# Attention of a fused RWKV, soft-MoE and feed-forward kernel rebuilt: one load per unit, natural keys by TensorE, decay table in PSUM, even and odd chunks as steps, w_in in quarters

## The chip, the cores and the metric

The kernel runs on one core of a Trainium2 chip. The metric is the device time of one execution in microseconds (us); the time given is the median of three runs.

## The reference, cut to what matters

Attention with a decaying state, then a soft mixture of experts, then a feed-forward block with squared ReLU. `w_in` and `w_out` come as float64, everything else as float32.

```python
# r, k, v: [4, 8, 768, 48]; w, u: [8, 48]
for t in range(S):
    cur = np.einsum('bhd,bhe->bhde', u[None] * kt, vt)
    y[:, :, t] = np.einsum('bhd,bhde->bhe', rt, state + cur)
    state = w[None, :, :, None] * state + np.einsum('bhd,bhe->bhde', kt, vt)
# x = y as [3072 tokens, 384]; 8 experts of 4 slots, F = 1024
logits = x @ phi
slot_input = softmax(logits over tokens).T @ x
slot_out[e] = relu(slot_input[e] @ w1[e]) @ w2[e]
x = softmax(logits over slots) @ slot_out
# d_ff = 2048
g = np.maximum(x @ w_in, 0) ** 2
out = g @ w_out
```

## The kernel before

**Units.** Attention is computed in 16 units, n = 0 to 15: one batch and a pair of heads each (four units make a batch). The 768 tokens of a unit are six chunks of 128. The turned arrays r and k of a unit lie with the head dimension on the partitions (head h at 64h to 64h+47), in `t_view`; the natural ones, k and r (`n_view`) and v (`vs`), with the tokens on the partitions. The host lays them out, and each comes by loads of its own: two of the turned arrays per unit (line 91), one of natural k and r (95), one of v (98), all on SP's queue from unit 1 on. Four units are in flight in `slot0` to `slot3`.

**One unit's work.** `decay` (231, VectorE) multiplies turned k and r by powers of w from the table `tab`. `prep` (238, 240, 242, GpSimd) forms r·u·k and weighs natural k with `pkn`. `weigh` (246, VectorE) sums r·u·k over a head's dimension, `diag` (253, GpSimd) spreads the sums on a diagonal in `AT`. `A` (263, TensorE) makes the products of k and r within a chunk, and a masked copy (265, VectorE) puts their upper triangles into `AT`. `KV` (274) makes k v per chunk, `scan` (280, VectorE) runs the state over the chunks, and ScalarE copies it into the block-diagonal `SBD` (284). `Y` adds state times r (294, full array, both heads at once) and `AT` times v (299). `X` (310, 311) transposes the result into `xn`, `L` (320) gives the logits. A unit is done in two steps g of three chunks each. At a batch's end `soft1a` to `soft3` and `softc` follow.

**Float64 to float32.** `to_f32` (137, 139, 141) takes the two words of a float64 apart in three VectorE instructions. All of `w_in` is loaded (146) and converted within the attention loop, 16 blocks of 128 x 384, at one block a unit (`conv_win`). `w_out` is loaded (154) and converted (to `wf`) and split into two fp32r parts (612, 617) during the expert stage and the first feed-forward steps.

**Order.** Instructions are issued in the order in which the program writes them (a manual schedule); each engine works in that order, and semaphores tie them. Seven expert weights (176, 179) are loaded in the loop in slots 6 to 12, four more in the units' slots as the last units end.

**Behind the loop.** A pass over the softmax of the last batch, then eight experts (`up` 556, `turn` 566, `down` 574), then `G` (678) and `quarters` (695) make the feed-forward's first factor `gst`; quarters 512 to 2047 go through `gq` and SP's transfers (708) to their partitions. Then come 96 steps i of nine matrix instructions (805), with `s_h` (722), `s_relu` (734, ScalarE), `s_sq` (739 ScalarE, 741 VectorE), `s_hi` (744, ScalarE), `s_lo` (747, VectorE) two and one steps ahead; step i belongs to f = i // 2 modulo 16.

Of the kernel before, what the change touches and what calls it, by code (L numbers as in the profile page):

```python
# [17 lines left out]
def rwkv_softmoe_ffn(ctx: ExitStack, tc: tile.TileContext, tr, kr, vn, wt, u, phi, w1, w2, w_in, w_out, out):  # L30
    nc = tc.nc
    NU, _, D, _, S = tr.shape
    NP = wt.shape[1]
    H = 2 * NP
    B = NU // NP
    NC = S // 128
    DM, NTOK = out.shape
# [47 lines left out]
    def n_view(n):

        return units[n % NB][:, 2 * S:2 * S + 4 * NC * D].rearrange("p (m c h d) -> p m c h d", m=2, c=NC, h=2)

    def load_t(n, engs, cols=slice(0, NC)):
        for h in range(2):  # L90
            engs[h].dma_start(t_view(n)[64 * h:64 * h + D, :, cols],
                              tr[n, h].rearrange("d m (c t) -> d m c t", c=NC)[:, :, cols])

    def load_n(n, eng=nc.sync):
        eng.dma_start(n_view(n).rearrange("p m c h d -> p m (c h d)"), kr[n].rearrange("p m c h d -> p m (c h d)"))

    def load_v(n, eng=nc.sync):
        eng.dma_start(vs[n % NV].rearrange("p c h d -> p (c h d)"), vn[n].rearrange("p c h d -> p (c h d)"))

    base = const.tile([112, 8], F32, name="base")  # L100
    nc.sync.dma_start(base[:, :NP], wt)
    nc.vector.memset(units[0][32:64, :2 * S], 0.0)
    load_t(0, (nc.sync, nc.scalar), slice(0, GC))
    load_n(0)
    load_t(0, (nc.sync, nc.scalar), slice(GC, NC))
    U = att.tile([128, NP, 2, D], F32, name="U")
# [313 lines left out]
    for j in range(3):  # L420
        prep(1, j)
# [444 lines left out]
```

## Time and profile before

| | us |
|---|---|
| median of three runs | 455.57 (453.97 to 457.31) |
| span of the profiled execution | 451.8 |
| PE busy | 397.7 |
| DVE busy | 308.9 |
| ACT busy | 209.2 |
| POOL busy | 135.0 |

The span is one execution from its first to its last instruction, taken by the hardware profiler; the median also holds what lies around it. PE is the matrix part of TensorE, PEld its weight loads, DVE VectorE, ACT ScalarE, POOL GpSimd, SP the queue that issues most loads. A busy time is an average over stages that are bounded by different things, so it has to be read by stage. fp32 matrix products appear as two instructions each, transposes as one. The granted clock is a share of 2.4 GHz.

### The profile page before, as it was taken

The numbers are of one execution on the slowest core, as the hardware profiler recorded it, in microseconds if no ns is written. First come the engines' busy times: TensorE is split into PE (matmuls) and PEld (weight loads), VectorE is DVE, ScalarE is ACT, GpSimd is POOL, SyncE is SP. The second block draws the span as 40 slices with busy tenths as digits, with TensorE's granted clock in tenths as the row PEclk, the third lists the DMA queues.
The fourth block names the chain that finished last, engine by engine and source line by source line (L and its number), as shares of the span: only waits on it lengthen the run. The fifth ranks groups of instructions, "written<-read, shape, count | busy, mean of one in ns | idle before, by whom it ended". The sixth has DMA issues, their size and how long they took to land.

```text
span 451.8 us, 7475 instructions
## 1 busy us (share of the span) xinstructions
PE 397.7 (88%) x2917; PEld 300.9 (67%) x2917; DVE 308.9 (68%) x525; ACT 209.2 (46%) x390; POOL 135.0 (30%) x114
## 2 busy tenths in 40 slices
PE   3687747986598699899999999999999999999996
PEld 2565534764276466444788888888888888888884
DVE  6888997999898772424766575676555667555564
ACT  3142221332134334212598888665555565555553
POOL 7896772577279760000122122000000000000000
PEclk9699996969599889999999999999999999999999
DMA  7989997699749987997243220030000012000004
GB/s 196 265 241 307 296 323 176 191 312 299 213 94 316 303 311 244 316 390 265 83 128 104 72 89 16 1 140 1 0 0 2 0 42 100 0 1 0 0 2 140
DMA packets 28516, 67.59 MB, mean 150 GB/s; under 512 B 2848, under 2 KB 12832, under 8 KB 28480
## 3 DMA queue, kind: packets, MB, share of 16 engines
q1 hardware_dynamic: 28112, 66.61, 48.4%
q10 hardware_dynamic: 368, 0.49, 0.5%
q8 instruction: 23, 0.38, 0.3%
q14 instruction: 13, 0.11, 0.1%
HBM read 61.59 MB, written 4.72 MB: 147 GB/s over the span
## 4 chain that ended last, share of the span: by engine, by line
PE 69%; DVE 14%; issue 4%; POOL 3%; DMA 2%; ACT 2%; SPq 0%; DVEq 0%; ACTq 0%; POOLq 0%
PE ps_A L805 22%; PE ps_lg L805 7%; PE ps_kv L805 7%; PE ps_Y L805 7%; PE ps_tr L722 5%; DVE AT L265 3%; DVE slot L231 3%; PE ps_Y L299 3%; PE ps_A L263 3%; DVE slot L139 2%; PE ps_Y L574 2%; PE ps_A L556 2%; PE ps_A L376 2%; DMA slot<-in_w_in_dram 2%; DVE dg L246 1%
## 5 line engine op out<-in xcount | busy, mean ns | idle before, releaser
L747 DVE TENSOR_TENSOR slot<-gg,slot 128x512 fp32r<-128x512 f32 (+1 forms) x97 | 66.5, 686 | 65.8 <-ACT slot L744 65.1
L805 PE MATMUL ps_A<-slot,slot 128*128 128x512 f32 x432 | 108.4, 395 | 0.0
L805 PEld LDWEIGHTS ps_A<-slot,slot 128*128 128x128 f32 x432 | 81.0, 188 | 19.4
L744 ACT CAST slot<-gg 128x512 fp32r<-128x512 f32 (+1 forms) x97 | 59.7, 616 | 50.7 <-DVE gg L741 49.9
L734 ACT ACTIVATE hr<-ps_tr 128x512 f32<-128x512 f32 (+1 forms) x97 | 57.5, 594 | 24.7 <-PE ps_tr L722 24.3
L741 DVE TENSOR_TENSOR gg<-hr 128x512 f32<-128x512 f32 (+1 forms) x71 | 48.9, 689 | 15.3 <-ACT hr L734 15.2
L805 PE MATMUL ps_lg<-slot,slot 128*128 128x512 f32 x144 | 56.0, 396 | 0.0
L805 PE MATMUL ps_Y<-slot,slot 128*128 128x512 f32 x144 | 56.0, 395 | 0.0
L805 PE MATMUL ps_kv<-slot,slot 128*128 128x512 f32 x144 | 55.9, 395 | 0.0
L253 POOL TENSOR_SCALAR_AFFINE_SELECT AT<-dg 128x768 f32<-128x768 f32 x32 | 34.2, 1070 | 49.8 <-DVE dg L246 47.7
L617 POOL TENSOR_TENSOR slot<-wf,slot 128x384 fp32r<-128x384 f32 x16 | 17.6, 1101 | 97.4 <-ACT slot L612 93.5
L231 DVE TENSOR_TENSOR slot<-slot,tab 112x768 f32<-112x768 f32 (+1 forms) x34 | 43.4, 1285 | 0.0
L299 PE MATMUL ps_Y<-AT,vs 128*48 128x128 f32 (+1 forms) x384 | 33.8, 291 | 10.1 <-DVE AT L265 9.8
L284 ACT COPY SBD<-sc 48x240 f32<-48x240 f32 x32 | 20.1, 629 | 43.4 <-DVE sc L280 43.2
L722 PE MATMUL ps_tr<-slot,slot 128*128 128x512 f32 x96 | 37.8, 395 | 0.0
L299 PEld LDWEIGHTS ps_Y<-AT,vs 128*48 128x48 f32 (+1 forms) x384 | 23.0, 134 | 17.9 <-DVE AT L265 14.9
L265 DVE COPY_PREDICATED AT<-mask,ps_A 128x384 f32<-128x384 int32 x64 | 33.5, 575 | 1.8 <-issue 1.6
L263 PE MATMUL ps_A<-slot 48*128 48x128 f32 x384 | 33.8, 315 | 0.0
L805 PEld LDWEIGHTS ps_Y<-slot,slot 128*128 128x128 f32 x144 | 27.0, 188 | 6.5
L805 PEld LDWEIGHTS ps_kv<-slot,slot 128*128 128x128 f32 x144 | 27.0, 188 | 6.4
L805 PEld LDWEIGHTS ps_lg<-slot,slot 128*128 128x128 f32 x144 | 27.0, 187 | 6.3
L240 POOL TENSOR_TENSOR slot<-slot 128x576 f32<-128x576 f32 x16 | 29.9, 1869 | 1.3
(154 smaller groups left out, 511.2 us busy)
## 6 DMA issues: line engine op xcount, KB each, us to landing
slot<-in_w_dram SPq DMA_DIRECT2D x14, 1536.0 KB, 12.9
slot<-in_kr_dram SPq DMA_DIRECT2D x16, 576.0 KB, 9.1
slot<-in_tr_dram SPq DMA_DIRECT2D x30, 288.0 KB, 8.6
slot<-in_w_in_dram SPq DMA_DIRECT2D x8, 768.0 KB, 10.0
wo<-in_w_out_dram SPq DMA_DIRECT2D x16, 384.0 KB, 3.1
vs<-in_vn_dram SPq DMA_DIRECT2D x16, 288.0 KB, 7.9
out_dram<-os SPq DMA_DIRECT2D x15, 256.0 KB, 2.1
post<-in_w_dram SPq DMA_DIRECT2D x2, 1536.0 KB, 8.4
```

What stands on the lines that cost most here:

```text
L231: eng.tensor_tensor(x, x, tab[:, n % NP, m].unsqueeze(1).to_broadcast([112, k_, 128]), ALU.mult)
L240: eng.tensor_tensor(rv, rv, kv, ALU.mult)
L253: nc.gpsimd.affine_select(out=at.rearrange("p c h t -> p (c h) t"), in_=dg.rearrange("p c h -> p (c h)").unsqueeze(2).to_broadcast([128, 2 ...
L263: nc.tensor.matmul(p[h][:, i], tv[rows, 1, GC * g + i], tv[rows, 0, GC * g + i], start=True, stop=True)
L265: nc.vector.copy_predicated(at[:, :, h], mask.unsqueeze(1).to_broadcast([128, GC, 128]), p[h])
L299: nc.tensor.matmul(p[64 * h:64 + D * h, i], vv[:, GC * g + i].rearrange("p h d -> p (h d)")[:, cols], at[:, i, h], start=False, stop=True, ...
L722: nc.tensor.matmul(p, gst[:, 128 * f:128 * (f + 1)], cTall[:, 512 * g:512 * (g + 1)], start=True, stop=True)
L734: nc.scalar.activation(fs[i, "hr"][:, c], fs[i, "p"][:, c], AF.Relu)
L741: nc.vector.tensor_mul(gg, hr, hr)
L744: nc.scalar.copy(part(i, "gh")[:, c], fs[i, "gg"][:, c])
L747: nc.vector.tensor_tensor(part(i, "gl")[:, c], fs[i, "gg"][:, c], fs[i, "gh"].bitcast(F32)[:, c], ALU.subtract)
L805: nc.tensor.matmul(o, (hi, lo, hi)[k][:, 128 * j:128 * (j + 1)], (gh, gh, gl)[k], start=(f == 0 and k == 0), stop=(f == NF - 1 and k == 2))
```

## The change

- The host joins turned r and k, natural r and natural v of a unit in one array `un` of 128 partitions x 2688 floats, three pieces of 896, zeros in the gaps. One DMA loads a unit; for unit 0 the three pieces go on three instructions (ScalarE's queue and SP's).
- Natural k is no longer loaded (except `k0` for unit 0, from GpSimd's queue): `kT` transposes the decayed turned k on TensorE, and ScalarE copies it to `kn`. The table factor that this carries is taken out of u instead (`UT`); the product with `pkn` goes.
- The table lies in PSUM, in one bank, and one half is read in reverse.
- A step is the even or the odd chunks of a unit. `A` writes one tile of two banks, and one masked copy of 768 elements does the work of two of 384. `SBD` and its copies go: `inter` multiplies the scanned state head by head (48 rows, 48 columns, 20 instructions for 10), `intra` does what line 299 did. Two Y banks stay allotted, and `X` writes its transposes into them. `L` has six products of 128 columns for three of 256.
- The softmax of a batch is spread over the first three units of the next; some of its copies go from VectorE to ScalarE; `xn` is doubled.
- `w_in` is loaded in quarters of 512 columns. Quarter 0 is converted in units 4 to 8, quarter 1 in the last units, quarters 2 and 3 in feed-forward steps 0 to 17, one instruction a step; their products (`quarters`) are made in steps 11 and 19, with 16 small transfers each.
- Weights in the loop are loaded in pieces of a third, `w2` is laid out by the host in runs of 4 KB.

The diff, cut to its core:

```diff
+    load_unit(0, (nc.scalar, nc.sync, nc.sync))
+    k0n = att.tile([128, NC, 2, D], F32, name="k0n")
+    nc.gpsimd.dma_start(k0n.rearrange("p c h d -> p (c h d)"), k0)
...
+    def conv_some(k):
+        for _ in range(k):
+            if conv:
+                q, c, i = conv.pop(0)
+                to_f32(win(q)[:, c], raws[q][:, c].rearrange("p (f t) -> p f t", t=2), (i,))
...
+    tabp = ps("tab")[:112].rearrange("p (a e) -> p a e", a=NP)
...
+    def decay(n, m, cols=slice(0, NC)):
         x = t_view(n)[:, m, cols]
+        t = tabp[:, n % NP, ::-1] if m else tabp[:, n % NP]
+        nc.vector.tensor_tensor(x, x, t.unsqueeze(1).to_broadcast(list(x.shape)), ALU.mult)
...
+    def kT(n, j):
+        tv = t_view(n)
+        p = ps("tr")[:, :HC * 128].rearrange("p (c e) -> p c e", c=HC)
+        for i in range(HC):
+            nc.tensor.transpose(p[:, i, :112], tv[:, 1, HC * j + i], ident[:112, :112])
         if j == 0:
+            st[n, "kn"] = wk([128, NC, 2, D], "kn", 2, pool=att)
+        nc.scalar.copy(st[n, "kn"][:, HC * j:HC * (j + 1)], heads(p))
...
+    def cp(n, par):
+        nc.vector.copy_predicated(st[n, "AT", par], mask.unsqueeze(1).unsqueeze(1).to_broadcast([128, 2, HC, 128]),
+                                  st.pop((n, "A", par)))
...
+    def inter(n):
+        sc, tv = st.pop((n, "sc")), t_view(n)
+        for c in range(1, NC):
+            par = c % 2
             for h in range(2):
+                o = 64 * (h ^ par)
+                rows = slice(64 * h, 64 * h + D)
+                nc.tensor.matmul(y_view(par)[o:o + D, c // 2], sc[rows, :, c], tv[rows, 0, c], start=(c < 3), stop=True,
+                                 skip_group_check=True)
...
+        if nxt:
+            pr2(n + 1)
+        A(n, 1)
+        if nx2:
+            decay(n + 2, 1)
+        cp(n, 1)
+        if n > 0:
+            L(n - 1, 1)
+            X(n - 1, 1)
+            if hp == 0:
+                soft1a(prev)
+        if nxt:
+            KV(n + 1)
+            scan(n + 1)
+        if nx2:
+            pr1(n + 2)
+            kT(n + 2, 0)
+        inter(n)
+        if n > 0 and hp == 0:
+            soft1b(prev)
+        if nxt:
+            weigh(n + 1)
+            diag(n + 1, 0)
+        intra(n, 0)
+        if nx2:
+            kT(n + 2, 1)
+            decay(n + 2, 0)
+        if nxt:
+            A(n + 1, 0)
+            cp(n + 1, 0)
+            diag(n + 1, 1)
+        if n > NP - 1:
+            if hp == 0:
+                soft2(prev)
+            elif hp == 1:
+                softc(prev)
+            elif hp == 2:
+                soft3(prev)
+        intra(n, 1)
+        L(n, 0)
+        X(n, 0)
+        if n >= 4:
+            conv_some(2)
+        if n + NB < NU:
+            load_unit(n + NB)
...
+        if n == NU - 5:
+            conv_some(9)
+            load_win(1, 5)
+            conv_add(1)
...
+    load_win(2, 5)
+    load_win(3, FREE[7])
...
-        if i in (0, 2, 4):
-            quarter_out(1 + i // 2)
+        if i == 0:
+            conv_add(2)
+        if i == 9:
+            conv_add(3)
+        if i < 18:
+            conv_some(1)
+        if i in (11, 19):
+            quarters(2 + i // 19, "tr")
+            quarters_high()
+            quarters_low()
+            for j in range(NQ):
+                quarters_out(2 + i // 19, j)
```

## Rows read from the trace of the kernel before

**Rows 1.** Stretches: bounds, length, busy us (instructions) by engine, clock, DMA share, GB/s.

```profile
core 0: us, PE busy (x) PEld busy (x) DVE busy (x) ACT busy (x) POOL busy (x), PEclk, DMA share, GB/s
...
24.78:173.16 148.38, 114.32 (x1311) 83.65 (x1309) 129.09 (x202) 44.85 (x96) 97.23 (x71) 0.88 0.89 261
...
223.20:265.10 41.90, 41.90 (x184) 33.76 (x183) 28.19 (x53) 37.64 (x67) 10.05 (x9) 1.00 0.32 95
```

**Rows 2.** The same view for a plain unit, a batch's end and a late unit.

```profile
40.65:51.12 10.47, 7.90 (x92) 5.65 (x90) 10.33 (x15) 2.92 (x6) 7.26 (x6) 1.00 1.04 329
...
61.91:78.53 16.62, 9.36 (x85) 5.67 (x84) 12.88 (x24) 4.01 (x9) 8.25 (x7) 0.69 0.86 263
...
164.08:170.40 6.32, 6.32 (x95) 5.18 (x91) 5.44 (x8) 3.04 (x7) 4.28 (x5) 1.00 0.74 244
```

**Rows 3.** Groups by line: engine, operation, out<-in, count; busy us, mean ns; idle before.

```profile
L231 DVE TENSOR_TENSOR slot<-slot,tab 112x768 f32<-112x768 f32 x30 | 40.7, 1361 | 0.0
...
L265 DVE COPY_PREDICATED AT<-mask,ps_A 128x384 f32<-128x384 int32 x64 | 33.5, 575 | 1.8 <-issue 1.6
...
L139 DVE SCALAR_TENSOR_TENSOR slot<-slot,slot 128x384 int32<-128x384 int32 x16 | 14.9, 933 | 0.6
L141 DVE SCALAR_TENSOR_TENSOR slot<-slot,slot 128x384 int32<-128x384 int32 x16 | 14.4, 897 | 0.5
...
L280 DVE TENSOR_TENSOR_SCAN sc<-ps_kv,carry 112x288 f32<-112x288 f32 x16 | 12.0, 749 | 10.2 <-PE ps_kv L274 5.5 <-issue 2.6 <-ACT xT L303 2.1
L246 DVE TENSOR_REDUCE dg<-slot 128x12 f32<-128x576 f32 x16 | 11.9, 743 | 2.8 <-POOL slot L240 2.8
...
L137 DVE TENSOR_SCALAR slot<-slot 128x384 int32<-128x384 int32 x16 | 7.1, 443 | 2.1 <-DMA slot<-in_w_in_dram 2.1
```

**Rows 4.** Timeline of DVE and POOL: start, duration, engine, line, operation, idle before.

```profile
42.25 2.20 POOL L240 TENSOR_TENSOR slot<-slot 128x576 f32<-128x576 f32 x1
...
43.36 1.52 DVE L139 SCALAR_TENSOR_TENSOR slot<-slot,slot 128x384 int32<-128x384 int32 x1
...
48.46 0.56 DVE L139 SCALAR_TENSOR_TENSOR slot<-slot,slot 128x384 int32<-128x384 int32 x1
...
68.98 0.94 DVE L231 TENSOR_TENSOR slot<-slot,tab 112x768 f32<-112x768 f32 x1
```

**Rows 5.** Timeline of PE in the late unit.

```profile
164.08 0.94 PE L263 MATMUL ps_A<-slot 48*128 48x128 f32 x12
164.95 0.51 PE L310 MATMUL ps_tr<-ident,xT 112*128 112x112 f32 x3
165.29 0.82 PE L294 MATMUL ps_Y<-slot,SBD 112*112 112x128 f32 x6
166.04 0.87 PE L299 MATMUL ps_Y<-AT,vs 128*64 128x128 f32 x12
166.84 0.94 PE L263 MATMUL ps_A<-slot 48*128 48x128 f32 x12
...
169.85 0.62 PE L274 MATMUL ps_kv<-vs,slot 128*48 128x48 f32 x20
170.40 0.94 PE L263 MATMUL ps_A<-slot 48*128 48x128 f32 x12
```

**Rows 6.** Timeline of PE: A at the low clock, soft3 at the full one.

```profile
156.75 1.65 PE L263 MATMUL ps_A<-slot 48*128 48x128 f32 x12
...
183.27 1.50 PE L376 MATMUL ps_A<-xn,en 128*32 128x385 f32 x12 [0.20 <-DVE m L508]
```

**Rows 7.** Stretches within one unit: DMA share and GB/s are the last two columns.

```profile
44.00:47.00 3.00, 1.48 (x11) 0.94 (x9) 2.97 (x5) 0.40 (x1) 3.00 (x3) 1.00 1.01 415
47.00:51.00 4.00, 3.45 (x53) 3.08 (x53) 3.93 (x7) 0.48 (x1) 0.87 (x2) 1.00 1.06 213
```

**Rows 8.** Timeline of the feed-forward steps: SP's transfers, DVE waiting for ACT.

```profile
229.07 2.41 SPq L708 DMA_DIRECT2D slot<-gq  x4
...
231.06 0.69 DVE L747 TENSOR_TENSOR slot<-gg,slot 128x512 fp32r<-128x512 f32 x1 [1.52 <-ACT slot L744]
```

More of the change, by code (lines that the diff above doesn't have):

```diff
@@ L89, in load_t @@
[L89 to L98, printed above, removed]
@@ L124, in rwkv_softmoe_ffn, with win @@
+    st = {}
+    warm = const.tile([1, 4], F32, name="warm")
+    nc.gpsimd.memset(warm, 1.0)
+    nc.scalar.activation(warm[:, 0:1], warm[:, 1:2], AF.Exp)
     w_in32 = w_in.bitcast(I32)
     w_out32 = w_out.bitcast(I32)
-    raw = [t[:, 1536 * h:1536 * (h + 1)].rearrange("p (c f) -> p c f", c=3)
-           for t in (take(NSLOT - 2, I32), take(NSLOT - 1, I32)) for h in range(2)]
-    win = [take(i).rearrange("p (c f) -> p c f", c=3) for i in (4, 5)]
+    winslot = take(4)
+    raws = {}
+    def win(q):
+        return winslot[:, 1536 * (q % 2):1536 * (q % 2 + 1)].rearrange("p (c f) -> p c f", c=3)
@@ L131, in to_f32, with load_win @@
+    def load_win(q, slot, cs=range(3)):
+        if q not in raws:
+            raws[q] = take(slot, I32).rearrange("p (c f) -> p c f", c=3)
+        for c in cs:
+            nc.sync.dma_start(raws[q][:, c], w_in32[128 * c:128 * (c + 1), 1024 * q:1024 * (q + 1)])
     def to_f32(dst, words, steps=range(3)):
@@ L219, in keep_clock @@
+    xn = [att.tile([128, NC, DM + 1], F32, name=f"xn{i}") for i in range(2)]
     def keep_clock(n):
@@ new lines, in rwkv_softmoe_ffn @@
+    nc.scalar.copy(carry[:, :, :, 1:], pw[:, 1, :, 0].unsqueeze(2).unsqueeze(3).to_broadcast([112, NP, D, NC - 1]))
+    KV(0)
+    for par in range(2):
+        nc.vector.memset(YB[par][32:64, :HC * 128], 0.0)
+    cp(0, 0)
+    scan(0)
+    diag(0, 1)
+    uw = wk([112, NP], "uw", 1, pool=att)
+    rsc = wk([112, NP, 128], "xT", 2, pool=att)
+    nc.vector.tensor_mul(uw, base[:, :NP], base[:, NP:])
+    nc.vector.tensor_tensor(rsc, tabp, uw.unsqueeze(2).to_broadcast([112, NP, 128]), ALU.mult)
@@ L422, in rwkv_softmoe_ffn @@
-    for m in range(2):
-        decay(1, m)
-    loads = [[("win", n)] if n < NF // 2 else [] for n in range(NU - NB)]
-    for i, n in enumerate((1, 3, 5, 7, 9, 10, 11)):
-        loads[n].append(("w", i))
-    conv = []
+        nc.tensor.transpose(pp[:, a * 128:a * 128 + 112], rsc[:, a], ident[:112, :112])
+    nc.scalar.copy(UT, heads(pp.rearrange("p (a e) -> p a e", a=NP)))
+    for m in (1, 0):
+        decay(1, m)
+    pr1(1)
+    kT(1, 0)
+    kT(1, 1)
+    nc.gpsimd.memset(xn[0][:, :, DM:DM + 1], 1.0)
@@ L428, in rwkv_softmoe_ffn @@
+    nc.gpsimd.memset(xn[1][:, :, DM:DM + 1], 1.0)
+    loads = [[] for n in range(NU)]
+    pieces = [("w", 0, c) for c in range(3)] + [("x", 0, c) for c in range(3)]
+    pieces += [("w", i, c) for i in range(1, NEARLY) for c in range(3)]
+    for j, pc in enumerate(pieces):
+        loads[min(NU - NB - 1, j * (NU - NB) // len(pieces))].append(pc)
     for n in range(NU):
         nxt = n + 1 < NU
+        nx2 = n + 2 < NU
+        prev = n // NP - 1
+        hp = n % NP
         if n == 2:
@@ L767, in rwkv_softmoe_ffn @@
     quarters_low()
-    quarter_out(0)
+    for j in range(NQ):
+        quarters_out(1, j)
     s_sq(1)
```

458 lines of the change are left out of this document (197 added, 261 removed).

## The prediction

> **What bounds the kernel now.** Read the table of stretches first [rows 1]. The attention loop, from A of unit 1 (24.78 us) to A of the last unit (173.16 us), takes 148.4 us, 10.60 us for each of 14 units. DVE is busy for 129.09 us of it (87%), PE for 114.32, POOL for 97.23, and the 16 DMA engines for 0.89 of it at 261 GB/s. The granted clock there is 0.88. In the feed-forward steps (223.20 on) PE is busy throughout at the full level, 2.4 GHz, and DVE for 28.19 of 41.90. So the change must win in the loop and must not disturb the steps.
>
> Next, three single units [rows 2]. In a plain unit (40.65 to 51.12) DVE works 10.33 of 10.47 us: it is the bound. In a unit at a batch's end (61.91) 16.62 us go by, DVE works 12.88, PE 9.36, and the clock falls to 0.69. In a late unit, in which nothing is prepared or converted any more (164.08), PE works all 6.32 us: that is what PE needs for a unit today at the full clock.
>
> What DVE does is in [rows 3]: per unit two decays of 1361 ns, four masked copies of 575, one weigh (743), one scan (749) and the three steps of one conversion (443, 933, 897). The timeline says that some of these durations are waiting [rows 4]: the same L139 takes 1.52 us while POOL's L240 runs and 0.56 when POOL is idle; a decay takes 0.94 us at best. The masked copy, which reads one operand from PSUM, keeps its 575 ns throughout.
>
> **What the change costs and saves, DVE.** Decays: with the table in PSUM they read one SBUF operand, as the masked copy does. Bounds 0.94 and 1.36; I take the row they resemble, 0.95: 1.9 per unit, 0.8 less. Masked copies: two of 768 in place of four of 384; between 0.94 (the decay of 768 elements) and 2 x 0.575; I take 1.0, so 2.0. Weigh and scan stay: 1.5. Sum 5.4. Conversions: 16 blocks x 2.27 = 36.4 us fall to 17 steps of 512 elements within the loop (quarter 0 and eight steps of quarter 1). A step of 384 costs 0.76 on the mean, so 1.0 for 512; bounds 0.75 (0.56 scaled) and 2.0 (1.52 scaled). That is 17 us, 1.1 per unit. The softmax pieces cost 12.88 - 10.33 = 2.55 per batch, 0.6 per unit. DVE: 5.4 + 1.1 + 0.6 = 7.1 us per unit.
>
> **PE.** From start to start in the full-clock stretch [rows 5]: A of half a unit 0.87, transposes of half a unit 0.34, six instructions of L294 0.75, twelve of L299 0.80, KV 0.55; from 166.84 to 169.85, A, L, transposes, four of L294 and L299 leave 0.5 for L. New: kT, two more groups of transposes, 0.68 per unit. L294's ten full-array instructions (1.25) become twenty of 48 rows and 48 columns. No row shows these. At L299's rate (0.80 / 12 = 0.067) they cost 1.33; below it, the two row halves running side by side would give about 0.7; above it, at L294's rate of 0.125, 2.5. I take 1.33, as L299 has the same moving width and nearly the same weights. L has twice the instructions of half the width: 0.5 to 1.0, I take 0.65. Sum: 1.74 + 0.68 + 0.68 + 1.33 + 1.60 + 0.55 + 0.65 = 7.2. Per batch soft3, 1.50 at the full clock [rows 6], and two groups of transposes (0.3 each) add 2.1, so 0.5 per unit: 7.7.
>
> **The others.** ACT loses the SBD copies and gains two copies per unit; it has 2.92 of 10.47 busy [rows 2], so it hides them. POOL loses one product in three: 7.26 becomes about 5.3. Both are below PE. The two or three softmax copies per batch that go from DVE to ACT, the second xn and the zeroed rows of the Y banks are too small to count.
>
> **The unit.** PE at 7.7 and DVE at 7.1 are now close, and each waits for the other in order: kT(n+2) on PE needs a decay that stands behind the conversions on DVE, and behind kT wait inter and intra. In the whole loop today the bound engine is busy 87% of the time, in a plain unit 99%. I take 95%: 7.7 / 0.95 = 8.1 us per unit. Bounds: 7.3 (the twenty instructions half side by side, little waiting) and 8.9 (87%). The new order spreads a batch's softmax over three units, which is why I stay above 87%. The single two-bank A tile puts A and its masked copy in series: 2 x (0.87 + 1.0) = 3.7 us per unit, well within 8.1.
>
> **Loads.** A unit becomes 1.38 MB and two pieces of 0.52 MB go with it: 2.42 MB per unit. Today's rate swings between 415 and 213 GB/s at a full share [rows 7]; the slow stretch is where the turned arrays, 48 partitions each, land. The change makes them part of one load over 128 partitions with runs of 3.5 KB, so I take nearer to 415: 6 us per unit, hidden behind 8.1. At the loop's 261 / 0.89 = 293 GB/s it would be 8.3, still level.
>
> **Before the loop.** A of unit 1 starts at 24.78 today. POOL makes one product less for unit 1 (L240, of the same shape, took 2.20 us with its waits [rows 4]), the table needs no copies, and unit 0 comes on three queues. Against that, POOL issues five loads ahead of its first product; at SP's 0.6 us each [rows 8] that is 3 us, or nothing if unit 0 lands later still. I take 1.4 us earlier, bounds 3 either way. The pass after the loop and the expert stage keep their matrix work; w2 comes in runs of 4 KB in place of 1.5, and one conversion is left there: nothing.
>
> **Feed-forward.** Two quarters of w_in are now converted in steps 0 to 17: 18 instructions of 512 elements, 0.56 scaled to 0.75 at most, 13 us on DVE over the 41.90 of [rows 1] (18 steps of 2.33). DVE goes from 28.19 to 41. Of a pair of steps it idles 1.5 us waiting for ACT [rows 8], which takes up one of the two conversions; the other pushes back the wf words for which ACT waits. How far ahead of PE the operands are, no row here shows; I count 1 us for the whole. The quarters leave PE 24 matrix instructions twice within the steps and take fewer than before ahead of them: 1 us. Each quarter then needs 16 transfers at 0.6 us; the first four must land within three steps (7 us) and take 2.4 us to issue: just in time. In all +2; bounds 0 and +12 (nearly every conversion on the path).
>
> **Sum.** Against the profiled 451.8: -1.4 - 14 x (10.60 - 8.1) + 2 = 417.4. The median of the runs is 455.57, 3.8 above the span, which lies around it; so 421.2. In general 307.8 + 14 x (time per unit).
>
> **A rule against it.** In [rows 5] an instruction of L299 (weights for one column half) takes 0.067 us, one of L294 (the full array) 0.125. inter alternates between two row halves, and both write into one PSUM bank. The Trainium skill, TensorEngine Tiling (Array Packing), section Gotcha 1: PSUM Pressure, says that different row tiles cannot access the same PSUM bank at once; no run here shows it. That is the first rival.
>
> **Rivals.**
> First, inter runs one by one: 20 x (0.125 - 0.06) = 1.3 us more per unit, 9.4, hence 439. For it: both halves share a bank. Against: the partitions differ. Chance 0.12.
> Second, the feed-forward steps suffer: +12 rather than +2, 431. For it: DVE nearly full there and 16 small transfers per quarter. Chance 0.10.
> Third, the clock stays at the lower level, 1.2 GHz: A then takes 1.65 us against 0.94 [rows 5, 6], so 7.2 x 1.75 = 12.6 per unit, 484, slower. It decides from about half of the units on, since 14 x 0.5 x 5 = 35 us is the gain. For it: the clock fell to 0.69 in the unit at a batch's end, in which PE did 9.36 us of work in 16.62. Against: the plain unit (7.90 of 10.47) and the late one both had 1.00 [rows 2], and PE will have more to do in less time. Chance 0.02.
> Fourth, the loads become the bound: at 213 GB/s 2.42 MB take 11.4 us, 467; at 228 GB/s nothing is gained. Against: the slow stretches go with the 48-partition loads. Chance 0.03, and another 0.03 that a rate near 228 gives no change.
>
> **How the numbers follow.** My forecast, a unit of 7.3 to 8.9 us, has 0.70 and gives 410 to 432 by itself. From 408 to 440 the first two rivals are in, and some 0.85. About 1% is what a measurement of this kernel can tell from no change. The forecast and the first two rivals are faster by more: 0.92; within 1% 0.03; slower 0.05.
>
> **What would show it.** Right: A to A at about 8 us with PE busy over 90% at a clock near 1.00; decays at 0.95 to 1.0 us whatever POOL does; no DMA stretch below 300 GB/s under load; steps still 2.33 us long between 224 and 265. Wrong: inter's instructions at 0.125 us; DVE waiting for unit loads; PE gaps in steps 11 to 14 or 19 to 22, ended by gq's transfers; a clock below 0.9 in the loop.

## The result, and the profile after

| | before | after |
|---|---|---|
| median, us | 456.31 (453.97 to 457.31, four runs) | 434.06 (428.65 to 441.19, four runs) |
| ratio, 95% interval | | 0.9426 [0.9358, 0.9493] |
| span of the profiled execution, us | 451.8 | 426.9 |
| attention loop, A(1,1) to A(15,1), us | 148.4 | 117.3 |

Medians take in all executions; the ratio and its interval compare only those within 1.5% of the fastest of their kernel (428.65 and 432.00 after), so it is not the quotient of the medians. The sum of the prediction gave 421.2 us, its range was 408 to 440: faster, as forecast, but 13 us less so. A(n,par) is the A of unit n for even (0) or odd (1) chunks. Line numbers are those of the kernel shown; in the kernel after, decay is L218, the masked copy L263, kT L227, A L259, inter L289, intra L298, L L318, the step's products L827.

The table of stretches of the kernel after, which answers [rows 1, 2]: the loop, a plain unit, units 6, 10 and 13, and the first 41.9 us of the feed-forward steps.

```profile
core 0: us, PE busy (x) PEld busy (x) DVE busy (x) ACT busy (x) POOL busy (x), PEclk, DMA share, GB/s
...
29.68:147.01 117.33, 110.95 (x1612) 80.26 (x1611) 90.30 (x127) 39.61 (x102) 60.30 (x55) 0.96 0.79 290
...
44.05:51.23 7.18, 7.18 (x113) 5.41 (x112) 5.13 (x7) 2.46 (x6) 4.53 (x5) 1.00 0.94 342
...
66.24:80.27 14.03, 11.86 (x125) 7.47 (x124) 10.77 (x16) 3.67 (x9) 5.36 (x5) 0.76 0.48 175
...
103.29:112.83 9.54, 8.73 (x126) 5.81 (x125) 8.34 (x14) 3.10 (x8) 5.69 (x6) 1.00 0.71 257
...
127.52:139.27 11.75, 9.07 (x115) 6.67 (x114) 6.67 (x10) 2.43 (x7) 5.12 (x5) 0.85 0.63 256
...
193.28:235.18 41.90, 41.39 (x200) 32.92 (x199) 36.24 (x64) 35.98 (x65) 10.50 (x9) 1.00 0.37 121
```

A plain unit lasts 7.18 us, and PE works all of it; DVE, which worked 10.33 of 10.47 us before [rows 2], works 5.13. The bound has moved to PE. Units 6 and 13 stand out: together they are 11.4 us longer than two plain ones (1.4 of it is the matrix work of soft3 in unit 6), and in both PE idles for 2.2 to 2.7 us, then runs at half clock (granted 0.51 from 71.5 to 78.5 us, 0.50 from 133.5 to 136.3). The time of a loop is not fixed: that of the sixth experiment below has the same instructions and took 8.4 us longer in its profile, with units 13 and 14 at 12.5 and 12.7 us:

```profile
31.67:157.38 125.71, 120.33 (x1611) 85.75 (x1610) 90.41 (x127) 39.67 (x102) 59.43 (x54) 0.90 0.73 271
```

The groups of DVE in the loop, which answer [rows 3]:

```profile
L263 DVE COPY_PREDICATED AT<-mask,ps_A 128x768 f32<-128x768 int32 x28 | 28.7, 1026 | 19.1 <-PE ps_A L259 15.9 <-POOL AT L249 1.4 <-issue 1.2
L218 DVE TENSOR_TENSOR slot<-slot,ps_tab 112x768 f32<-112x768 f32 x26 | 24.5, 942 | 0.0
...
L139 DVE SCALAR_TENSOR_TENSOR slot<-slot,slot 128x512 int32<-128x512 int32 x5 | 5.1, 1025 | 0.1
```

Decays take 942 ns on the mean for 1361 (none in the loop more than 949), masked copies 1026 (1.0 us was forecast). A conversion step takes 0.81 us on the mean of its three instructions (1.0 was forecast); the one shown, L139, takes 1.03.

inter, in the timeline of PE:

```profile
32.35 0.35 PE L289 MATMUL ps_YO<-slot,sc 48*48 48x128 f32 x2
32.37 0.35 PE L289 MATMUL ps_YE<-slot,sc 48*48 48x128 f32 x2
32.54 0.28 PE L289 MATMUL ps_YO<-slot,sc 48*48 48x128 f32 x2
32.55 0.28 PE L289 MATMUL ps_YE<-slot,sc 48*48 48x128 f32 x2
...
33.18 0.43 PE L298 MATMUL ps_YE<-AT,slot 128*48 128x128 f32 x4
```

Twenty instructions take 0.83 us, 0.042 each, a third of L294's 0.125 [rows 5]: four start within 0.02 us.

Where the 24.9 us between the spans come from: until A(1,1) +4.9 (29.68 for 24.78), loop -31.0, from A(15,1) to the first expert -2.5 (12.03 for 14.54), expert stage +0.1, feed-forward +3.7 (from the first product of G, L694, at 188.81, to the end 238.1, for 234.4).

### The profile page after: what moved, and what is told of

It is laid out like the page before. It is cut to its first block, busy times and chain, and to the rows that moved or that the text cites. A ratio compares the mean times of both kernels' runs of the same rounds, so it can differ in the third digit from the quotient of the medians.

```text
span 426.9 us, 8177 instructions
## 1 busy us (share of the span) xinstructions
PE 396.1 (93%) x3303; PEld 298.2 (70%) x3303; DVE 281.2 (66%) x472; ACT 203.5 (48%) x402; POOL 95.6 (22%) x100
## 4 chain that ended last, share of the span: by engine, by line
PE 81%; DVE 6%; DMA 5%; issue 3%; ACT 2%; SPq 1%; POOL 1%; DVEq 0%; ACTq 0%; POOLq 0%
PE ps_A L827 20%; PE ps_Y L827 7%; PE ps_lg L827 7%; PE ps_kv L827 7%; PE ps_A L259 6%; PE ps_tr L733 4%; PE ps_tr L227 4%; PE ps_YE L298 3%; PE ps_YO L289 3%; DMA wo<-in_w_out_dram 3%; PE ps_Y L586 3%; PE ps_YO L298 2%; PE ps_A L568 2%; PE ps_lg L318 2%; PE ps_kv L271 2%
## 5 line engine op out<-in xcount | busy, mean ns | idle before, releaser
L827 PE MATMUL ps_A<-slot,slot 128*128 128x512 f32 x432 | 108.3, 395 | 0.0
L827 PEld LDWEIGHTS ps_A<-slot,slot 128*128 128x128 f32 x432 | 81.1, 188 | 19.1
L827 PE MATMUL ps_Y<-slot,slot 128*128 128x512 f32 x144 | 56.3, 398 | 0.0
L827 PE MATMUL ps_lg<-slot,slot 128*128 128x512 f32 x144 | 55.9, 395 | 0.0
L827 PE MATMUL ps_kv<-slot,slot 128*128 128x512 f32 x144 | 55.8, 394 | 0.0
L263 DVE COPY_PREDICATED AT<-mask,ps_A 128x768 f32<-128x768 int32 x32 | 32.8, 1024 | 24.3 <-PE ps_A L259 21.2
L259 PE MATMUL ps_A<-slot 48*128 48x128 f32 x384 | 32.2, 303 | 8.9 <-DVE slot L218 8.9
L249 POOL TENSOR_SCALAR_AFFINE_SELECT AT<-dg 128x768 f32<-128x768 f32 x32 | 27.3, 870 | 57.3 <-DVE dg L242 46.1
L259 PEld LDWEIGHTS ps_A<-slot 48*128 48x128 f32 x384 | 25.7, 200 | 13.7 <-DVE slot L218 8.9
L827 PEld LDWEIGHTS ps_kv<-slot,slot 128*128 128x128 f32 x144 | 27.1, 188 | 6.6
L827 PEld LDWEIGHTS ps_Y<-slot,slot 128*128 128x128 f32 x144 | 27.0, 188 | 6.4 <-issue 0.2
L827 PEld LDWEIGHTS ps_lg<-slot,slot 128*128 128x128 f32 x144 | 27.0, 188 | 6.1
L218 DVE TENSOR_TENSOR slot<-slot,ps_tab 112x768 f32<-112x768 f32 (+1 forms) x34 | 30.1, 896 | 0.7 <-DMA slot<-in_un_dram 0.7
L230 ACT COPY kn<-ps_tr 128x288 f32<-128x288 f32 x32 | 12.8, 401 | 24.4 <-PE ps_tr L227 24.2
L227 PE MATMUL ps_tr<-ident,slot 112*128 112x112 f32 x96 | 18.5, 309 | 6.2 <-issue 3.9
L234 POOL TENSOR_TENSOR slot<-slot,UT 128x576 f32<-128x576 f32 x15 | 22.2, 1477 | 4.0 <-ACT UT L420 3.3
```

Of the source, the lines that this page charges most:

```text
L218: nc.vector.tensor_tensor(x, x, t.unsqueeze(1).to_broadcast(list(x.shape)), ALU.mult)
L227: nc.tensor.transpose(p[:, i, :112], tv[:, 1, HC * j + i], ident[:112, :112])
L234: nc.gpsimd.tensor_tensor(rv, rv, UT[:, n % NP].unsqueeze(1).to_broadcast([128, NC, 2, D]), ALU.mult)
L249: nc.gpsimd.affine_select(out=at, in_=dg.unsqueeze(3).to_broadcast([128, 2, HC, 128]), pattern=[[0, 2], [0, HC], [1, 128]], compare_op=ALU ...
L259: nc.tensor.matmul(p[:, h, i], tv[rows, 1, 2 * i + par], tv[rows, 0, 2 * i + par], start=True, stop=True)
L263: nc.vector.copy_predicated(st[n, "AT", par], mask.unsqueeze(1).unsqueeze(1).to_broadcast([128, 2, HC, 128]), st.pop((n, "A", par)))
```

## The experiments

The theory: TensorE sets a unit (7.18 us), and what the change fails to give is lost in single stalls that the order on DVE makes, in the prologue (the work ahead of A(1,1)), and in the feed-forward conversions. The rivals stand in each expectation. Times are medians; ratios are to the kernel before.

**Unit 13: the conversion that waits for its load.** The rows of DVE and PE in unit 13 of the kernel after:

```profile
130.39 0.43 DVE L137 TENSOR_SCALAR slot<-slot 128x512 int32<-128x512 int32 x1 [3.40 <-DMA slot<-in_w_in_dram]
...
131.46 0.95 DVE L218 TENSOR_TENSOR slot<-slot,ps_tab 112x768 f32<-112x768 f32 x1
...
132.51 0.48 PE L227 MATMUL ps_tr<-ident,slot 112*128 112x112 f32 x3 [2.68 <-issue]
134.37 1.52 PE L298 MATMUL ps_YE<-AT,slot 128*48 128x128 f32 x12
```

The load of quarter 1 was issued at 120.77, behind a unit and two pieces of weights. DVE waits 3.40 us for it, the decay behind it comes late, and kT idles 2.68 us, put down to "issue". After that L298 takes 1.52 us, not 0.86.

```diff
         if n == NU - 5:
             conv_some(9)
             load_win(1, 5)
+        if n == NU - 3:
             conv_add(1)
```

> Only the point from which quarter 1 of w_in is converted is moved, from unit 12 to unit 14; the load is issued where it was. Theory 1 (the changed kernel loses its gain in single stalls of VectorE, after which the clock falls): in the profile after, L137 waits 3.40 us for this load at 130.39 us, kT of unit 15 starts 2.68 us late and unit 13 lasts 11.75 us where a plain one lasts 7.18. Without the wait, unit 13 falls to 7.2 to 7.8 us and the time by about 4 us (to some 0.990 of the changed kernel's). Rival (the wait is hidden, or the clock falls there for another reason): unit 13 stays above 10 us and the time does not move. Second rival: the five steps of conversion that are moved on into the expert stage cost there what is won here (no change of time, but unit 13 short).

Measured: 431.05 us, ratio 0.9365 [0.9278, 0.9452]. Its stretches, unit 1 and unit 13:

```profile
31.68:43.77 12.09, 12.09 (x113) 8.89 (x112) 5.31 (x7) 2.56 (x6) 4.54 (x5) 1.00 0.51 199
...
135.60:143.11 7.51, 7.51 (x116) 5.62 (x115) 5.22 (x8) 2.32 (x7) 5.04 (x5) 1.00 0.97 392
```

Unit 13 falls from 11.75 to 7.51: the wait made the stall, and without the wait the clock stays. From A(15,1) to the first expert the time is unchanged (12.03), so the moved steps cost nothing. The median falls by 3 us, but the intervals overlap, so a gain in the whole time is not shown. In the profiled execution what unit 13 wins is lost elsewhere: unit 1 takes 12.09 us for the same instructions. This is the prologue's matter (below).

**Unit 6: the order on DVE.** In the kernel after:

```profile
65.83 1.46 DVE L360 TENSOR_TENSOR cnat<-en,mx 128x192 f32<-128x192 f32 x1
...
67.33 0.36 ACT L361 ACTIVATE cnat<-cnat 128x192 f32<-128x192 f32 x1 [2.24 <-DVE cnat L360]
...
68.11 0.42 PE L318 MATMUL ps_lg<-xT,phs 112*32 112x128 f32 x6 [0.93 <-ACT xT L301]
...
68.81 0.69 DVE L141 SCALAR_TENSOR_TENSOR slot<-slot,slot 128x512 int32<-128x512 int32 x1
69.42 0.42 DVE L137 TENSOR_SCALAR slot<-slot 128x512 int32<-128x512 int32 x1
69.75 0.94 DVE L218 TENSOR_TENSOR slot<-slot,ps_tab 112x768 f32<-112x768 f32 x1
...
70.80 0.48 PE L227 MATMUL ps_tr<-ident,slot 112*128 112x112 f32 x3 [1.25 <-issue]
72.48 1.52 PE L298 MATMUL ps_YE<-AT,slot 128*48 128x128 f32 x12
```

Two stalls follow each other. softc's exponential on ACT (L361) waits for DVE, behind it the copy of xT, behind that PE (0.93 us). Then softc's sums and two conversion steps stand ahead of the decay for which kT waits (1.25 us). The second experiment takes away the conversions' part.

```diff
         cp(n, 1)
+        if n > 4:
+            conv_some(2)
...
-        if n >= 4:
-            conv_some(2)
```

> Only the order on VectorE is changed: the two conversion steps of a unit stand behind the odd masked copy of the next unit, no longer ahead of the decay for which kT waits. Theory 1: in unit 6 of the profile after (66.24 to 80.27, 14.03 us) kT waits 1.25 us for a decay that stands behind a conversion of 1.03 us, then the clock falls to half; with the conversion out of the way the unit falls to 7.2 to 9 us, and the time by some 5 us (0.988). Rival (the first stall of that unit, 0.93 us at 68.11, where ScalarE's copy of xT stands behind the softmax of the batch, is enough to let the clock fall): unit 6 stays above 12 us. For unit 13 both expect little: the wait for the load of 3.40 us stands in the unit wherever it is, though it may now meet the scan and not the decay.

Measured: 443.33 us, 0.9708 [0.9648, 0.9768], slower than the kernel after. Unit 6 falls to 9.93 us with the full clock, units 8 and 9 from 8.06 and 7.77 to 7.50 and 7.51. The theory holds in kind, and the rival (the first stall is enough) falls; the 9.93 lies above the 7.2 to 9 expected, in which soft3's 1.43 us was forgotten. But DVE now reaches the first step on quarter 1 at 116.60 us, 0.8 us after the load's issue; in the kernel after it came 6.2 us behind it:

```profile
65.79:75.72 9.93, 8.72 (x126) 5.81 (x125) 8.83 (x14) 3.58 (x9) 5.13 (x6) 1.00 0.68 248
...
124.97 0.43 DVE L137 TENSOR_SCALAR slot<-slot 128x512 int32<-128x512 int32 x1 [8.37 <-DMA slot<-in_w_in_dram]
...
131.69:144.86 13.17, 13.17 (x115) 9.38 (x115) 6.73 (x13) 3.13 (x8) 4.36 (x4) 0.50 0.36 123
```

Units 12 to 14 last 17.16, 13.17 and 12.68 us, the last two at about half clock (0.50 and 0.56) with PE busy throughout. I had expected little there; I had not counted how far the wait is brought forward.

**The table back in SBUF.**

```diff
+    tabs = att.tile([112, NP, 128], F32, name="tabs")
+    nc.scalar.copy(tabs, tabp)
...
-        t = tabp[:, n % NP, ::-1] if m else tabp[:, n % NP]
+        t = tabs[:, n % NP, ::-1] if m else tabs[:, n % NP]
```

> One part undone: the decay table is copied to SBUF once, and the decays read it there, as in the kernel before. All expect the decays to grow from 0.94 us to 1.2 to 1.4 us on the mean while GpSimd works, so 0.5 to 0.8 us more on VectorE per unit. Theory 1 (TensorE sets a plain unit, 7.18 us of 7.18 busy; VectorE works 5.1 to 5.5 of them): plain units stay at 7.2 us and the time moves by less than 1%, so the table in PSUM is not where the gain comes from. Rival (the decays stand on the path of every unit, since kT waits for them): 14 x 0.5 to 0.8 = 7 to 12 us slower (1.016 to 1.027).

Measured: 439.07 us, 0.9607 [0.9538, 0.9676]. The group of decays in its loop:

```profile
L220 DVE TENSOR_TENSOR slot<-slot,tabs 112x768 f32<-112x768 f32 x25 | 27.5, 1100 | 0.0
```

Plain units stay at 7.18 us, as theory 1 says; but the five units near a batch's end (5, 6, 8, 9, 10) are 0.85, 1.58, 1.10, 1.30 and 2.09 us longer than after, 6.9 in all. Unit 6 varies by itself (14.03 us after, 15.23 in the first experiment, with the same table), so its 1.58 may not be the table's; the other four repeat there to 0.02 us. So in this profile the table in PSUM is worth 5 to 7 us, all in units near a batch's end, in which DVE has more to do. In the ratios the version is 1.9% slower than the kernel after, which is the size that the rival gave (1.016 to 1.027), but not by its mechanism, in every unit. The decays grew less than all expected, to 1100 ns on the mean, single ones to 2157.

**inter by head.**

```diff
-        for c in range(1, NC):
-            par = c % 2
-            for h in range(2):
+        for h in range(2):
+            for c in range(1, NC):
+                par = c % 2
```

> Only the order of inter's twenty instructions is changed: ten of one head, then ten of the other, in place of pairs that use different halves of the rows. Theory 1 (the pairs run side by side, 0.042 us an instruction in the profile after, and TensorE sets the unit): without partners they take 0.067 us or more, 1.33 us in place of 0.83 for the twenty, a plain unit lasts 7.7 us and the time grows by about 14 x 0.5 = 7 us (1.016). If an instruction alone takes 0.125 us, as a full array's did before, it is 2.5 us, and 23 us more (1.05). Rival (an instruction of 48 columns takes 0.042 us alone): no change.

In its timeline of PE:

```profile
33.76 0.35 PE L289 MATMUL ps_YO<-slot,sc 48*48 48x128 f32 x1
33.76 0.35 PE L289 MATMUL ps_YE<-slot,sc 48*48 48x128 f32 x1
...
34.88 0.86 PE L298 MATMUL ps_YE<-AT,slot 128*48 128x128 f32 x12
```

The twenty take 1.12 us (0.056 each), and a plain unit 7.48: 0.30 more for 0.29 more. So PE sets the unit, to the hundredth, and the pairs of row halves gain. In the kernel after, a group of four follows the one before in 0.11 us (32.54 to 32.65). The size was off (1.33 expected): with one head at a time, instructions for different column halves still start together. Its times, 434.26 to 471.60, are too far apart for a ratio; their spread was not explained.

**Does idle time keep TensorE slow in the prologue?** In the kernel after:

```profile
9.95 1.40 POOL L391 TENSOR_TENSOR slot<-slot,U 128x576 f32<-128x576 f32 x1 [3.45 <-DMA slot<-in_un_dram]
...
20.28 1.65 PE L259 MATMUL ps_A<-slot 48*128 48x128 f32 x12
...
27.23 0.94 PE L259 MATMUL ps_A<-slot 48*128 48x128 f32 x12
```

From 20.28 on PE has no gap, but works at half rate until some 27 us. The column of the granted clock says 1.00 there, but this is no measurement: the first clock record of this trace stands at 27.15 us, and a stretch without a record is counted as 1.00. So it is with the row of unit 1 above. In the other versions profiled the first record, and with it the full rate, came between 26.2 and 52.3 us. In the kernel before there are records: full from 11.87, half from 15.29 to 22.11 us. That kernel ran three matrix instructions without use ahead of its first A; the change left them out.

```diff
+    def warm_up(n):
+        p = ps("lg")
+        for _ in range(n):
+            nc.tensor.matmul(p[:, :256], ident, ident.unsqueeze(1).to_broadcast([128, 2, 128]), start=True, stop=True)
...
     decay(0, 0, EV)
+    warm_up(5)
     A(0, 0)
...
+    warm_up(1)
     KV(0)
...
+    warm_up(2)
     pp = ps("lg")
```

> Eight additional matrix instructions without use (128 x 256, the form that the kernel before ran three times in its prologue) are put where TensorE is idle before unit 1: five ahead of the first A, one ahead of KV of unit 0, two ahead of the transposes for UT. Theory 1 (TensorE still runs at half rate, A 1.65 us in place of 0.94, until some time after it has been kept busy without a gap; in the profile after that lasted to 26.5 us, in the execution profiled with quarter 1 late to 43 us): with the gaps filled A(1,1), the second A of unit 1, starts no later than 28 us in any execution, units 1 and 2 last 7.18 us each, and the median falls by 3 to 8 us (0.982 to 0.993 of the changed kernel's), with less spread between runs. Rival (what sets unit 0 is the arrival of its data and the chain of VectorE and GpSimd; TensorE's rate there costs nothing): at most 1 us. Second rival: the additional instructions delay unit 0 by up to 2 us, and nothing is gained.

Measured: 435.26 us, 0.9459 [0.9370, 0.9548], no gain over the kernel after. PE in its profile:

```profile
2.73 4.63 PE L218 MATMUL ps_lg<-ident 128*128 128x256 f32 x10 [2.73 <-POOL ident masks.py:199]
...
27.18 1.65 PE L264 MATMUL ps_A<-slot 48*128 48x128 f32 x12
...
42.87 0.42 PE L323 MATMUL ps_lg<-xT,phs 112*32 112x128 f32 x6
```

The instructions fill most of the gaps (PE is busy 14.1 of the 17.5 us from 2.7 to 20.2; in the kernel after 6.7 of 18.3 from 2.0), yet the half rate lasts to 42.9 us. Theory 1 asked for A(1,1) by 28 us in any execution, and it came at 31.54. A prologue without any gap was not tried.

**The conversions in the feed-forward steps.** The idle time of PE in the steps of the kernel after, all of it:

```profile
214.96 0.66 PE L602 MATMUL ps_tr<-ident,cs 128*128 128x128 f32 x4 [0.51 <-ACT hr L745]
...
240.63 0.86 PE L705 MATMUL ps_tr<-slot,soT 128*32 128x128 f32 x24 [0.77 <-ACT hr L745]
242.44 0.66 PE L602 MATMUL ps_tr<-ident,cs 128*128 128x128 f32 x4 [0.95 <-ACT hr L745]
```

```diff
-        if i < 18:
-            conv_some(1)
```

> Left out: the conversion of quarters 2 and 3 of w_in in the feed-forward steps 0 to 17 (their products are made from the words that quarters 0 and 1 left in the tiles). The load and the small transfers stay. My step 'feed-forward +2' is that one conversion of two delays the operands (1 us) and the quarters cost 1 us. If so, the time falls by about 1 us. Rival 1 (the second rival of the prediction): the conversions cost up to 12 us. Rival 2: the loss of the feed-forward stage lies in the wait for the first w_out blocks at its start, which this leaves as it is: no change.

From the first step's products to the end: 231.88 us for 233.62 (233.6 to 235.7 in the other versions with these conversions). One wait is left:

```profile
252.35 0.65 PE L602 MATMUL ps_tr<-ident,cs 128*128 128x128 f32 x4 [0.71 <-ACT hr L745]
```

The conversions cost 1.74 us, of which 1.5 is PE idle because ACT is late. My term was 1, and rival 1's 12 is out. Before, this stretch took 228.6 us; of the 3.3 that are left the two quarters' products are 1.7 (0.86 each) and the wait 0.7; 0.9 stays open. The median, 435.79, shows none of it: in the profiled execution A(1,1) came 2.0 us later than in that of the kernel after, and the loop, which this edit does not touch, took 8.4 us longer (125.71, shown above).

**The order mended.**

```diff
         cp(n, 1)
+        if n > NP and hp == 1:
+            softc_a(prev)
+        elif n > NP and hp == 2:
+            softc_b(prev)
+        elif n == NU - 4:
+            conv_some(9)
+            load_win(1, 5)
+        elif n > 4:
+            conv_some(2)
...
             kT(n + 2, 0)
+        if n > NP and hp == 1:
+            softc_exp(prev)
...
-        if n >= 4:
-            conv_some(2)
...
-        if n == NU - 5:
-            conv_some(9)
-            load_win(1, 5)
+        if n == NU - 2:
             conv_add(1)
```

> All that stands ahead of a decay on VectorE without need is moved behind the odd masked copy of the next unit: the conversion steps (none in the units that do the softmax over slots), and that softmax, cut into three (sums and division one unit later). Quarter 1 of w_in is loaded in unit 12 and converted from unit 15 on. Theory 1 (the stalls are made by the order on VectorE): units 6, 10 and 13 last 7.2 to 8.0 us in place of 14.0, 9.5 and 11.8, the loop from A(1,1) to A(15,1) falls from 117.3 to 104 to 107 us, and the median by 10 to 13 us (0.970 to 0.977 of the changed kernel's). Rival (VectorE is near its bound in these units whatever the order, as its 10.77 busy us in unit 6 suggest): the stalls move into the next unit, and less than 4 us are gained.

Measured: 420.32 us (417.63 to 423.22), 0.9241 [0.9170, 0.9312]. The loop:

```profile
30.90:137.50 106.60, 106.05 (x1612) 77.54 (x1611) 83.25 (x121) 39.78 (x102) 58.33 (x54) 1.00 0.87 320
```

PE works 106.05 of 106.60 us at the full clock. Units 6, 10 and 13 last 8.61, 8.61 and 7.50 us; 1.43 of each 8.61 is soft3, which the 7.2 to 8.0 expected had left out. The theory holds, and this version beats both kernels. Three more versions on this order (the warm-up, unit 0's data first, the prologue's order, all below) show the same loop in their profiles, 106.59 or 106.60 us, where the order of the kernel after gave 117.3 to 125.7. The edit changes three things at once; the first two experiments show the shares of units 13 and 6, the rest is not taken apart.

With the warm-up instructions added:

> Both of the former together: the order on VectorE and the eight instructions for TensorE's clock in the prologue. Theory 1: the gains add, 13 to 20 us below the changed kernel, 414 to 421 us. Rival: the gains are the same low-clock time counted twice, and this is no better than the better one of the two.

Measured: 423.95 us, 0.9306 [0.9240, 0.9372]: no better than the order alone. PE reached its rate at 29.1 us, for 30.1 without.

**Unit 0's data first** (on the mended order):

```diff
+    gate = units[0][0:1, OT + ON:OT + ON + 1]
+    nc.scalar.copy(units[1][0:1, 0:1], gate)
     for n in range(1, NB):
         load_unit(n)
```

> The kernel with the changed order on VectorE (e7_order), and one thing more: a copy of one element on ScalarE lets the loads of units 1 to 3 start only when unit 0 has landed. My step 'prologue -1.4' came out at +4.9: GpSimd's first product waits until 9.95 us for natural r, whose transfer was issued by 2.2 us. Theory 1 (the loads of units 1 to 3, issued right behind, share the DMA engines with unit 0's last piece): the product starts 2 us earlier or more, A(1,0), the first A of unit 1, starts 2 to 3 us earlier than 20.16, and the time falls by 2 to 3 us against e7_order (420.3). Rival 1 (the first transfer takes that long by itself, or another wait comes next): less than 0.5 us. Rival 2 (unit 1 now lands too late for its decay at 16 to 18 us): slower by 1 to 4 us.

(The A at 20.16 us is the odd one of unit 0, not one of unit 1, as I wrote.) Measured: 419.46 us, 0.9235 [0.9167, 0.9302], not to be told from the mended order (0.9241). GpSimd's first product starts at 9.27 us for 9.82 there (the 9.95 is the kernel after's), that A at 19.61. In the chain of waits the transfer takes 7.38 us for 7.93: it takes that long nearly by itself, and the neighbours cost some 0.55. Of the 2 us and more that theory 1 expected, 0.55 came, near rival 1, and A(1,1) did not move at all (30.89 for 30.90): PE worked at half rate until 30.8.

**One block a unit back on DVE** (on the mended order):

```diff
         cp(n, 1)
+        if n > 0:
+            more_conv(n)
...
+    def more_conv(n):
+        words = v_view(n).bitcast(I32).rearrange("p c h d -> p (c h d)").rearrange("p (f t) -> p f t", t=2)
+        dst = wk([128, ON // 2], "mc", 1)
+        for i in (0, 1, 2, 2):
+            to_f32(dst, words, (i,))
```

> The kernel e7_order with additional work on VectorE: in each unit four conversion instructions of 288 elements into a tile that nothing reads, as many elements as the one block of w_in that the kernel before converted in a unit (three of 384). VectorE is busy 83.3 us of 106.6 in e7_order's loop, TensorE 106.1. Theory 1 (TensorE sets the loop only because most conversions were moved out; 2.0 to 2.8 us more on VectorE per unit bring it to 7.9 to 8.7 us): the loop grows from 106.6 to 113 to 122 us, 6 to 15 us more in all. Rival (VectorE had enough room; the move of the conversions was not needed): less than 2 us more.

```profile
29.23:164.09 134.86, 127.30 (x1612) 91.17 (x1611) 107.88 (x178) 40.07 (x102) 59.43 (x55) 0.82 0.69 253
```

The four instructions are 1.8 us a unit (450 to 458 ns each), 25 in all; DVE is still busy only 80% of the loop. In the profiled execution (447.02 us) the loop takes 134.9 us, 28.3 more than without. The four executions spread from 432.50 to 460.08 us, too far for a ratio; the lowest is 12 us above the mended order's median, within the 6 to 15 expected, their median (450.84) 30. So theory 1 is right on the sign, and its size is not settled. The first units that lengthen, 2 and 3, take 7.95 and 7.55 us for 7.18; later, where softmax and conversions come together, there are waits and the clock falls (0.82 on the mean; 0.52 from 125 us on).

**The turned arrays as 48-partition transfers** (on the mended order, from unit 4 on):

```diff
+        if n >= NB:
+            for o in (0, 64):
+                for q, f in ((0, NPC and PW), (1, OT - PW)):
+                    engs[0].dma_start(dst[o:o + D, q, :f], un[n, q, o:o + D, :f])
+            engs[0].dma_start(dst[:, 1, OT - PW:], un[n, 1, :, OT - PW:])
+            engs[0].dma_start(dst[:, 2], un[n, 2])
+        elif len(engs) == 1:
```

> The kernel e7_order, and from unit 4 on the turned arrays come as four transfers of 48 partitions each, as before, the natural ones as two of 128 partitions; all from the same array, 1.18 MB in place of 1.38 a unit, six issues in place of one. The fourth rival of the prediction put the slow stretches (213 GB/s at a full share) down to the 48-partition loads. If so: 2.2 MB a unit at 213 to 260 GB/s take 8.5 to 10.4 us, VectorE's decays wait for slots, and the loop takes 115 us or more in place of 106.6. Rival (the rate does not depend on the partitions; the slow stretch before had another reason): the loop stays at 106 to 108 us.

Measured: 424.37 us, 0.9237 [0.9144, 0.9331]. Its loop from unit 3 on:

```profile
54.93:147.20 92.27, 91.68 (x1388) 66.75 (x1387) 72.59 (x108) 34.81 (x90) 50.33 (x46) 1.00 0.99 287
```

Units last as long as without (7.19, 7.50, 8.61). The DMA engines are now busy 99% of the time at 287 GB/s, where the one load had 86% at 317 over the same units: these transfers are slower, but fewer bytes go, and PE still covers them. Whether that is for the 48 partitions, as I read from [rows 7], or for the shorter runs into which the edit also cuts the arrays (1.0 and 2.5 KB beside 3.5), is not shown. The load in one piece buys room, not time.

**The prologue's order** (on the mended order):

```diff
     kT(0, 1)
-    weigh(0)
-    diag(0, 0)
     nc.vector.memset(kvp[:, :D * NC], 0.0)
...
         nc.vector.memset(YB[par][32:64, :HC * 128], 0.0)
-    cp(0, 0)
-    scan(0)
-    diag(0, 1)
...
     nc.scalar.copy(UT, heads(pp.rearrange("p (a e) -> p a e", a=NP)))
+    weigh(0)
+    diag(0, 0)
...
+    cp(0, 0)
+    scan(0)
+    diag(0, 1)
```

> The kernel e7_order, and in the prologue the product for UT, its transposes, the zeroing of three PSUM banks and one small square are done by VectorE (2.0 us in all) while it waits 3.13 us for GpSimd ahead of weigh, not behind the scan. Theory 1 (behind the landing of unit 0, the prologue is one chain through GpSimd and VectorE, on which these stand without need): the second A of unit 0, at 20.16 us in e7_order, starts at 17.0 to 18.2, and the time falls by 2 to 3 us against e7_order's 420.3 (to about 418). Rival (unit 1's decay is then held up by unit 1's transfer, or TensorE's half rate lasts longer by as much): less than 1 us.

Measured: 421.20 us, 0.9271 [0.9216, 0.9325]: no gain. The A starts at 19.42 us, 0.74 earlier, though natural r came 0.31 later. In its timeline:

```profile
14.79 1.01 DVE L263 COPY_PREDICATED AT<-mask,ps_A 128x768 f32<-128x768 int32 x1 [0.98 <-POOL AT L249]
```

The masked copy, at 14.75 us with the mended order, waits for GpSimd's diagonal instead: what went from DVE's path only uncovered that of GpSimd. Neither theory nor rival named it; the rival's size is right. A(1,1) came at 28.76 us in this profile, 2.1 earlier, with the half rate ended at 26.2 us and not at 30.0; the median shows no such gain.

## Why the prediction was right, and where it was off

The 13 us are five differences: prologue +6.3, loop +4.0, end of the loop -2.5, feed-forward +1.7 (9.5 for the span), and the median, which lies 7.2 us above the profiled span and not 3.8. The last is no step of the mechanism: I took a profile's span for a typical one, and the profile of the kernel after is of its 428.65 us execution. In two other profiles of a loop with the same instructions it took 125.7 us, units 13 and 14 longer by half clock; that the other executions lost their time so is likely, not shown.

The time came out within the range, but the forecast by itself gave 410 to 432. The range reached to 440 for the sake of the first two rivals, and both fell: that 434 lies in it is luck.

*The bound moves from DVE to PE: right, shown.* PE's sum of 7.2 us met 7.18. The terms were off in both directions, and that they cancel is luck: inter 0.83 for 1.33, four groups of transposes 0.43 each for 0.34, L 0.70 for 0.65. inter by head shows that PE's time goes into the unit one to one. With softmax I had 7.7; the mended order gives 106.6 / 14 = 7.61.

*DVE 7.1 us: too high.* It was 90.3 / 14 = 6.45. Decays at 0.94 and masked copies at 1.03 were right; fourteen steps of conversion at 0.81, not 17 at 1.0, fell into the loop.

*The coupling, 95%: the step that failed in the loop.* I took the waits as a share of every unit, 8.1 - 7.7 = 0.4 us, 5.6 us in 14 units. They are zero in plain units and sit in a few: 6, 10 and 13 hold 13.8 us above 3 x 7.18, of which 2.9 is soft3's work twice and the rest waits and half clock. I had named the cause (the decay behind the conversions), but not that a conversion would wait for its load; and I had priced the low clock only as a state of half the units or more (the third rival), not as some us behind a single wait. The order mended recovers 10.7 us of the loop, nearly twice the term.

*What the change is worth by part.* Moving the conversions out is the largest part measured: one block a unit put back (on the mended order) costs 12 us by the lowest time and 28.3 in the loop of the profiled execution, for the 31 that the loop gained. The table in PSUM gives 5 to 7, the joined load nothing yet.

*The prologue, -1.4: the step with the wrong sign.* I bounded the transfer of unit 0 at "nothing if it lands later still" and did not price its landing: GpSimd's first product starts 1.35 us later than before (9.95 for 8.60). UT's transposes and kT of unit 1 then lengthen the chain, and the half rate of PE, which I had priced from [rows 5, 6] for the loop alone, lasts 7 us into gapless work. From A(0,1) to A(1,1) it costs at least 9.40 - 7.2 = 2.2 us in this execution; in the one with quarter 1 late 4.1 there and 4.9 in unit 1. That difference is of the size of the spread between runs. Why it ends at 27 us in one execution and at 43 in another stays open; filling most of the idle time before 20 us did not end it sooner. GpSimd's first product before, for the 9.95 shown above:

```profile
8.60 1.54 POOL L238 TENSOR_TENSOR slot<-slot,U 128x576 f32<-128x576 f32 x1 [1.59 <-DMA slot<-in_kr_dram]
```

*Feed-forward, +2: +3.7.* The conversions cost 1.74 for 1, as measured. The quarters' products were counted as 1: they cost 1.7 within the steps, a wait of 0.7 with them, and give back 1.3 ahead of the steps. 0.9 stays open. *End of the loop, nothing: -2.5.* Why it is shorter was not looked into.

*What would show it.* PE was busy 95% of the loop at a clock of 0.96, the decays kept 0.93 to 0.95 us whatever GpSimd did, DVE waited for no unit load, and a plain step lasts 2.33 us: right. A to A is 8.38 us on the mean, near the 8.1, but no unit is of that kind: most last 7.2 to 8.1, three 9.5 to 14. Two of the three gaps stand ahead of step 19's products, where I had named a gap as a sign of an error, one ahead of step 9's; but ACT ends them, not gq's transfers.

*The rivals.* The first fell: inter ran at 0.042 us. The rule that I weighed there (the Trainium skill, TensorEngine Tiling (Array Packing), section Gotcha 1: PSUM Pressure: different row tiles cannot access one PSUM bank at once) does not show here as a cost: two instructions into YO start within 0.01 us at 32.35, and I read them as the two heads', since both halves of the rows write that bank for an odd chunk; with pairs the twenty take 0.83 us, one head at a time 1.12. The second fell: the conversions cost 1.74 us. The third, in full, fell (0.96 in the loop), but its mechanism is what units 6 and 13 lost by. The fourth fell: at 99% share the loads were still covered. In the kernel after, 4 us stretches of the loop at a share of 0.95 or more moved 332 to 425 GB/s.

## What to carry to other kernels

When a change moves the bound to another engine, price what stands ahead of each hand-over on the old one, in order: an instruction that waits for a load, ahead of one for which the new bound waits, costs its wait and then the clock (in unit 13, a wait of 3.40 us for the load cost 4.2). Before costing such coupling as a share of every stage, go through the stages that differ from the plain one. Put work that nobody awaits behind the hand-over, and check when its data land there too.

## What the runs showed of the hardware that I had not expected

- At a kernel's start the column of the granted clock can read 1.00 for want of a record while TensorE runs at half rate: unit 1 took 12.09 us with PE busy throughout, for 7.18 with the same instructions, in a trace whose first clock record stands at 42.91 us. Only durations of single instructions show it.
- In unit 6 of the kernel after, two gaps of 0.93 and 1.25 us were followed by 6.8 us at half clock, in unit 13 one of 2.68 us by 3.4; in the second experiment two shorter gaps in unit 6 (0.59 and 0.62 us) were followed by none.
- Four products of 48 rows and 48 columns start within 0.02 us, 0.042 us an instruction.
